# Attention block in BF16: the Q weights as one load, the safe program between two parts of each engine's code

## The chip, the cores and the metric

The kernel runs on one core of one Trainium2 chip. The metric is the device time of one execution in microseconds, lower is better. Three executions of the kernel before gave 420.71, 427.15 and 420.68 us; their median is 420.71.

## What is computed

One attention block without a mask: S = 2048 rows, D = 448, H = 16 heads of 28 columns, everything in bfloat16.

```python
qkv = (x @ wqkv).reshape(B, S, 3, H, Dh).transpose(2, 0, 3, 1, 4)
q, k, v = qkv[0], qkv[1], qkv[2]
scores = einsum("bhqd,bhkd->bhqk", q, k) * Dh ** -0.5
p = softmax(scores, axis=-1)
o = einsum("bhqk,bhkd->bhqd", p, v)
return o.transpose(0, 2, 1, 3).reshape(B, S, D) @ wo
```

## The kernel before

Two whole programs are written into the kernel. The fast one (`_fast`) leaves out the subtraction of the row maximum in the softmax and checks at the end, from the reciprocals of the row sums, that this was safe; it writes the answer as a flag of one number. The safe one (`_general`) subtracts the maximum. It stands behind the fast one in every engine's code and is run only when the flag says so. With the inputs given it never runs.

**The fast program.** Heads are taken four at a time (groups g = 0 to 3) and queries 512 at a time (chunks c = 0 to 3), which gives 16 units u, group by group. For a unit and a block kt of 128 keys there are four tiles of scores, one for each head, 128 x 512. PE computes scores into PSUM (operations S, line 854). ACT takes the exponential of two or three tiles in one instruction (E, line 877), and DVE takes the tiles that are left over by a polynomial in six steps (D1 to D6, lines 899 to 919). PE multiplies the four tiles of a block with V (operations PVu_kt, line 810), which also sums the rows. A unit's result is copied from PSUM (ACCEV), its row sums go through DRAM and back over SP's queue (L1 to L4, lines 722 to 731), and DVE scales the result (NM, line 733). The chunks of the last group are multiplied with wo (OP, line 703), copied (OPEV, lines 689 and 691) and stored (ODMA, line 693). For the last unit, `last_unit` does this without DRAM: the parts of wo of the first three groups are multiplied ahead (OPA, line 752, three matmuls for each of the four row tiles 12 to 15), then come two small transposes and broadcasts by matmul (N1, N2, lines 771 and 786), the scaling (line 791), and the fourth part (OPB, line 795). ACT copies and stores tiles 12 and 14, DVE and SP tiles 13 and 15. The check is a small matmul (CKS, line 947) and an instruction on DVE (FLAG, line 950).

**The order.** A planner (`_Prog.schedule`) simulates the five engines with estimated durations and puts every operation in a fixed place of its engine's stream. Among those that can start it takes the one with the lowest `prio`. Filler matmuls on zeros (Z, line 463) go where PE would otherwise do too little. `emit_engine` writes the streams out, with semaphore waits.

**The start.** x comes in four chunks and wqkv in the parts K, Q, V. Loads are issued by SP and ACT, each in its own queue (lines 424 and 427). PE transposes x (line 527; `tr_job`), DVE or ACT copies the result (xT, lines 511 and 515), and PE projects Q and K of the first group (line 544, `proj_qk`, four passes `it` of four matmuls for each) before the first scores.

**The end.** Each engine waits for the flag, loads it, and branches over the safe program to a block `done_...`, where SP waits for the stores. A hint for the branch (`mark_branch_hint_location`) is written some operations ahead, in front of the operation that `HINT_AT` names. These are the lines:

```python
hint = F.emit_engine(e, eng, fs)
eng.wait_ge(fs["dve"], F.flag_op.count)
ok = eng.value_load(F.flag_ap)
eng.br_ne(ok, 0, on_true=f"done_{e}", on_false=f"safe_{e}").branch_hint(hint)
```

Of the kernel before, what the change touches and what calls it, by code (L numbers as in the profile page):

```python
# [62 lines left out]
class _Prog:  # L63
# [12 lines left out]
    WINDOW = 3413.0  # L76
    FILL = None
    HINT_AT = {}
    FILL_DUR = 235.0
    FILL_ACT = 512.0  # L80
    FILL_TARGET = 5600.0
# [202 lines left out]
                    c += 1  # L284
                    op.count = c

    def emit_engine(self, e, engine, sems):
        waited = {}
        hint = None
        for op in self.order[e]:  # L290
            if op.name == self.HINT_AT.get(e):
                hint = engine.mark_branch_hint_location()
            need = {}
            for d in op.deps:
                if d.dma_group is not None:
                    key = ("dma", id(d.dma_group))
                    val = 16 * d.dma_index
                    sem = d.dma_group.sem
                else:
                    key = ("eng", d.eng)  # L300
                    val = d.count
                    sem = sems[d.eng]
                if waited.get(key, 0) >= val:
                    continue
# [10 lines left out]
        return engine.mark_branch_hint_location() if hint is None and self.HINT_AT else hint  # L315


RLO = 2.0 ** -40
# [18 lines left out]
def _fast(nc, x, wqkv, wo, out, n_heads=16):  # L337
# [32 lines left out]
    P = _Prog()  # L370
    es = ExitStack()
    with es:
# [196 lines left out]

        for c in range(NCH):  # L570
            for it in range(NIT):
                tr_job(4 * c, it, -3 + 0.001 * it if c == 0 else 0.25 * c - CFG["klead"] + 0.001 * it, "act" if (c == 0 and it == 1) else "dve")
# [168 lines left out]
        def last_unit(u, last_pv):  # L741
            g, c = units[u]
            ub = u % 2
            pr = u - 50.0
            open_ops = []
            for j in range(NQT):
                n = c * NQT + j
                hold = []

                for gg in range(G - 1):  # L750
                    def f_part(e, n=n, hold=hold, gg=gg):
                        return e.matmul(bank(hold[0].banks[0])[:, 0:D], OTN[:, gg, n * 128:(n + 1) * 128], wop[:, gg, :],  # L752
                                        start=(gg == 0), stop=False, skip_group_check=True)
                    op = P.add("pe", f_part, deps=([otn_ev[(g_, c)] for g_ in range(G - 1)] + dma_wo[-1:] + mid_ev) if gg == 0 else [], after=hold[-1:], kind="f", units=0.9, act=448.0,
                               prio=-34.0, name=f"OPA{n}_{gg}", acq=("T", 1) if gg == 0 else None)
                    if gg == 0:
                        hold.append(op)
                open_ops.append((n, hold, op))
            HF = QCH // 2
            evs = []  # L760
            for k in range(2):
                sl = slice(k * HF, (k + 1) * HF)
                evs.append(P.add("dve", (lambda e, sl=sl: e.tensor_copy(OTS[:, ub, sl], bank(pv_open[u].banks[0])[:, sl])),
                                 deps=[last_pv, ots_last[ub]], after=evs[-1:], dur=340, prio=pr, name=f"ACCEV{u}_{k}", rel=[(pv_open[u], 0)] if k else []))
            n1s, rss, n2s, nms = [], [], [], []
            for k in range(2):
                def f_n1(e, k=k):
                    b = n1s[k].banks[0]
                    ins = None
                    for qt in (2 * k, 2 * k + 1):  # L770
                        ins = e.matmul(bank(b)[:, qt * 4:(qt + 1) * 4], OTS[:, ub, qt * 128:(qt + 1) * 128], SEL[:, :], start=True, stop=True)  # L771
                    return ins
                n1s.append(P.add("pe", f_n1, deps=[evs[k], sel_op], after=n1s[-1:], dur=430, prio=pr, name=f"N1_{u}_{k}", acq=("T", 1)))
            for k in range(2):
                i0 = u * 16 + 8 * k
                rss.append(P.add("dve", (lambda e, k=k, i0=i0: e.reciprocal(RS[:, i0:i0 + 8], bank(n1s[k].banks[0])[:, 8 * k:8 * k + 8])),
                                 deps=[n1s[k]], after=rss[-1:], dur=120, prio=pr, name=f"RS{u}_{k}", rel=[(n1s[k], 0)]))
                rs_last.append(rss[-1])

# [13 lines left out]
            for j, (n, hold, op) in enumerate(open_ops):  # L793
                def f_fin(e, n=n, hold=hold):
                    return e.matmul(bank(hold[0].banks[0])[:, 0:D], OTN[:, g, n * 128:(n + 1) * 128], wop[:, g, :], start=False, stop=True, skip_group_check=True)  # L795
                fin = P.add("pe", f_fin, deps=[nms[j // 2]], after=[op], kind="f", units=0.9, act=448.0, prio=pr, name=f"OPB{n}")
                out_tile(n, fin, hold[0], "act" if j % 2 == 0 else "dve", pr)

        def pv(u, kt):
# [790 lines left out]
def _mha(nc, x, wqkv, wo, out, n_heads=16):  # L1590
# [3 lines left out]
    with es:  # L1594
# [11 lines left out]
        block = es.enter_context(nc.Block())  # L1606

        def body(e, eng):
            hint = F.emit_engine(e, eng, fs)
            eng.wait_ge(fs["dve"], F.flag_op.count)  # L1610
            ok = eng.value_load(F.flag_ap)
            eng.br_ne(ok, 0, on_true=f"done_{e}", on_false=f"safe_{e}").branch_hint(hint)
            with nc.body(f"safe_{e}", valid_engines=[eng.engine]):
                if e == "sp":
                    for gr in F.finish:
                        eng.wait_ge(gr.sem, 16 * gr.n)
                eng.drain().then_inc(bar, 1)
                eng.wait_ge(bar, 5)
                R.emit_engine(e, eng, rs)
                if e == "sp":  # L1620
                    for gr in R.finish:
                        eng.wait_ge(gr.sem, 16 * gr.n)
                eng.br(f"done_{e}")
            nc.switch_bb(f"done_{e}")
            if e == "sp":
                for gr in F.finish:
                    eng.wait_ge(gr.sem, 16 * gr.n)
# [52 lines left out]
```

## Time and profile before

| what | value |
|---|---|
| median of three executions | 420.71 us |
| the execution with the profile | 424.5 us |
| its span, from the first to the last instruction | 422.7 us |
| mean granted clock of TensorE | 0.996 |
| ACT busy | 402.9 us (95%) |
| DVE busy | 385.5 us (91%) |
| PE busy | 380.2 us (90%) |
| moved by DMA | 10.28 MB |

The profile belongs to one execution, whose own time is 424.5 us; 1.8 us of it lie outside its span. Times inside the span count from its first instruction. PE is the matmul engine, PEld its weight load, DVE the vector engine, ACT the scalar engine, POOL GpSimd, SP the engine that issues most DMAs; a q behind the name marks the engine's sequencer, which works through waits, branches, hints and DMA issues. A row of the timeline has start, duration, engine, line, operation, the tile written and the tile read, shapes, count, and in brackets the idle time before it with what ended it. Line numbers are those of the kernel before.

### The profile page before, as it was taken

Reading aid. Unit: us, or ns where it says so; the run is one execution under the profiler, and the core shown is the slowest. Engines: PE = TensorE matmul, PEld = TensorE weight load, DVE = VectorE, ACT = ScalarE, POOL = GpSimd, SP = SyncE. Lnnn points to the kernel's source line nnn. Section 1 sums busy time; section 2 is a strip of 40 time slices with the busy share of each in tenths; the row PEclk is TensorE's granted clock in tenths of the full one; section 3 lists DMA queues with packets and bytes.
Section 4 is the critical chain, followed back from the end, with each engine's and each line's share of the span. In section 5 each row is a group of like instructions: output and inputs, shape, how many; then the busy total and the mean of one; then the engine's idle time right before and its main releaser. Section 6 shows DMA issues by size and latency. Waiting matters only on the chain.

```text
span 422.7 us, 9986 instructions
## 1 busy us (share of the span) xinstructions
PE 380.2 (90%) x4419; PEld 122.4 (29%) x4419; DVE 385.5 (91%) x608; ACT 402.9 (95%) x312; POOL 3.4 (1%) x9
## 2 busy tenths in 40 slices
PE   6999898899999898998989899989989998898895
PEld 3433222322323223232322222223222322222232
DVE  4489999999999999999999999999999999999923
ACT  2799999999999999999999999999999999999991
POOL 3000000000000000000000000000000000000000
PEclk9899999999999999999999999999999999999999
DMA  8200000101010000100001010000000001100111
GB/s 262 65 2 2 5 26 3 27 0 29 2 26 5 4 26 2 29 2 18 13 3 27 2 28 2 4 26 4 27 2 27 2 6 25 36 28 24 59 44 51
DMA packets 13897, 10.28 MB, mean 24 GB/s; under 512 B 5980, under 2 KB 11868, under 8 KB 13848
## 3 DMA queue, kind: packets, MB, share of 16 engines
q1 hardware_dynamic: 12808, 8.72, 7.6%
q10 hardware_dynamic: 1040, 0.86, 0.6%
q8 instruction: 36, 0.59, 0.6%
q14 instruction: 13, 0.11, 0.1%
HBM read 7.50 MB, written 2.08 MB: 23 GB/s over the span
## 4 chain that ended last, share of the span: by engine, by line
ACT 93%; PE 3%; DMA 2%; DVE 0%; ACTq 0%; issue 0%
ACT PT L877 93%; DMA w_raw<-in_wqkv_dram 2%; PE ps L544 1%; PE ps L752 1%; PE ps L854 0%; PE ps L810 0%; PE ps L527 0%; PE ps L795 0%; PE ps L703 0%; PE ps L771 0%; PE ps L463 0%; DVE OUTS L691 0%; PE ps L786 0%; ACTq L427 0%; ACTq L424 0%; DVE OTN L791 0%
## 5 line engine op out<-in xcount | busy, mean ns | idle before, releaser
L877 ACT ACTIVATE PT<-ps 128x1536 bf16<-128x1536 f32 (+1 forms) x307 | 399.4, 1797 | 2.5 <-PE ps L854 2.5
L854 PE MATMUL ps<-QT,KT 28*128 28x512 bf16 x1024 | 152.5, 384 | 31.4 <-ACT PT L877 28.2
L463 PE MATMUL ps<-ZM,ZW 128*32 128x512 bf16 x1404 | 113.8, 388 | 1.4 <-DVE ZM L445 1.2
L810 PE MATMUL ps<-PT,V 128*32 128x512 bf16 x890 | 96.0, 388 | 2.3 <-DVE OTS L716 1.1
L899 DVE TENSOR_SCALAR DT<-ps 128x512 f32<-128x512 f32 x134 | 91.3, 684 | 2.7 <-PE ps L854 1.5
L854 PEld LDWEIGHTS ps<-QT,KT 28*128 28x128 bf16 x1024 | 37.4, 91 | 164.9 <-ACT PT L877 130.8
L919 DVE SCALAR_TENSOR_TENSOR PD<-DT,DU 128x1024 int16<-128x1024 f32 x67 | 81.7, 1219 | 1.2
L810 PE MATMUL ps<-PD,V 128*32 128x512 bf16 x134 | 50.9, 388 | 0.0
L917 DVE TENSOR_TENSOR DU<-DU,DW 128x1024 f16<-128x1024 f16 x67 | 46.2, 689 | 1.7
L913 DVE TENSOR_TENSOR DU<-DW 128x1024 f16<-128x1024 f16 x67 | 46.0, 686 | 1.5
L911 DVE TENSOR_SCALAR DW<-DT 128x1024 f16<-128x1024 uint16 x67 | 45.5, 680 | 0.2
L463 PEld LDWEIGHTS ps<-ZM,ZW 128*32 128x32 bf16 x1404 | 34.7, 96 | 37.3 <-issue 19.9
L810 PEld LDWEIGHTS ps<-PT,V 128*32 128x32 bf16 x890 | 23.9, 93 | 51.5 <-issue 39.0
L544 PE MATMUL ps<-xT,w_raw 112*32 112x512 bf16 x512 | 35.3, 390 | 2.0 <-DMA w_raw<-in_wqkv_dram 1.8
L915 DVE TENSOR_SCALAR DU<-DU 128x1024 f16<-128x1024 f16 x67 | 27.9, 416 | 0.8
L515 DVE CAST KT<-ps 128x512 bf16<-128x512 f32 x16 | 11.0, 685 | 7.6 <-PE ps L544 7.4
L561 PE MATMUL ps<-w_raw,xT 112*128 112x112 bf16 x256 | 16.4, 214 | 0.2 <-DVE DT L899 0.2
L544 PEld LDWEIGHTS ps<-xT,w_raw 112*32 112x32 bf16 x512 | 11.5, 97 | 16.4 <-issue 3.5
L691 DVE CAST OUTS<-ps 128x448 bf16<-128x448 f32 x14 | 8.7, 622 | 7.2 <-PE ps L703 6.6
L561 PEld LDWEIGHTS ps<-w_raw,xT 112*128 112x128 bf16 x256 | 12.9, 98 | 5.9 <-issue 4.2
L810 PEld LDWEIGHTS ps<-PD,V 128*32 128x32 bf16 x134 | 12.1, 93 | 7.8 <-issue 6.6
L703 PE MATMUL ps<-wop,OTN 128*128 128x448 bf16 x48 | 11.3, 355 | 0.0
(47 smaller groups left out, 96.0 us busy)
## 6 DMA issues: line engine op xcount, KB each, us to landing
RB<-scr_r SPq DMA_DIRECT2D x60, 64.0 KB, 2.0
out_dram<-OUTS SPq DMA_DIRECT2D x14, 112.0 KB, 1.7
x_nat<-in_x_dram SPq DMA_DIRECT2D x3, 448.0 KB, 8.9
w_raw<-in_wqkv_dram SPq DMA_DIRECT2D x2, 196.0 KB, 5.3
w_raw<-in_wqkv_dram ACTq DMA_DIRECT2D x2, 196.0 KB, 5.7
w_raw<-in_wqkv_dram SPq DMA_DIRECT2D x1, 392.0 KB, 9.6
wop<-in_wo_dram SPq DMA_DIRECT2D x16, 24.5 KB
scr_l<-OTS SPq DMA_DIRECT2D x15, 8.0 KB
```

The source lines that it names most:

```text
L463: ins = e.matmul(ps[32 * h:32 * h + 32, b * 512:(b + 1) * 512], ZW[:, :], ZM[:, :], start=shut, stop=shut, skip_group_check=not shut, tile ...
L544: ins = e.matmul(ps[32 * h:32 * h + 32, b * 512:(b + 1) * 512], w_raw[0:IT, it, col:col + 32], xT[0:IT, it, c * 512:(c + 1) * 512], start= ...
L561: ins = e.matmul(ps[:, b * 512 + j * GD:b * 512 + (j + 1) * GD], xT[0:IT, it, n * 128:(n + 1) * 128], w_raw[0:IT, it, 2 * D + g * GD:2 * D ...
L810: ins = e.matmul(ps[32 * h:32 * h + 32, b * 512:(b + 1) * 512], V[:, kt, hh * 32:(hh + 1) * 32], p_ap, start=(kt == 0), stop=(kt == NK - 1 ...
L854: ins = e.matmul(bank(b), KT[32 * h:32 * h + rows, g, kt * 128:(kt + 1) * 128], QT[32 * h:32 * h + rows, g, c * QCH:(c + 1) * QCH], start= ...
L877: ex = P.add("act", (lambda e, p0=p0, w=w, bf=bf: e.activation(PT[:, p0 * 512:(p0 + w) * 512], bank(bf(), w), AF.Exp, scale=ESCALE)), deps ...
L899: o1 = P.add("dve", (lambda e, T1=T1, s=s: e.tensor_scalar(T1, bank(s.banks[0]), ZLO, ZOFF, ALU.max, ALU.add)), deps=[s, d_last[di]], dur= ...
L911: o2 = P.add("dve", (lambda e, F16=F16, W=W: e.tensor_scalar(W, F16, ES, EC, ALU.mult, ALU.add)), deps=[o for _, o, _ in pair] + [d_last[d ...
L913: o3 = P.add("dve", (lambda e, W=W, U=U: e.tensor_tensor(U, W, W, ALU.mult)), deps=[o2], dur=65 + n * 0.521, prio=pr, name=f"D3_{gi}")
L915: o4 = P.add("dve", (lambda e, U=U: e.tensor_scalar(U, U, EP, None, ALU.add)), deps=[o3], dur=65 + n * 0.261, prio=pr, name=f"D4_{gi}")
L917: o5 = P.add("dve", (lambda e, W=W, U=U: e.tensor_tensor(U, U, W, ALU.mult)), deps=[o4], dur=65 + n * 0.521, prio=pr, name=f"D5_{gi}")
L919: o6 = P.add("dve", (lambda e, U=U, T=T, O=O: e.scalar_tensor_tensor(O, T, ZFIN, U, ALU.add, ALU.add)), deps=[o5] + [slot_last.get(("D", q ...
```

## The change

1. The Q part of wqkv is no longer split over the two queues. It is one load of 392 KB on SP's queue, issued behind SP's half of the K part and ahead of the second chunk of x.
2. The second tile of the first transposed chunk (xT, `it` = 1) is copied by DVE, as the other three, not by ACT. The projection of K gets a lower `prio` than that of Q. As the planner places it, PE does the four K passes first and then the four Q passes; before, one K pass, four of Q and three of K.
3. At the end, `prio` of OPA goes from -34.0 to -34.9, and that of the last two OPB from -35 to -34.8. PE's order behind the two OPB of tiles 12 and 13 was OPB14, CKS, OPA15 (three), OPB15; now it is OPA15 (three), OPB14, OPB15, CKS. On DVE the copy of tile 15 now stands in front of FLAG.
4. The safe program no longer stands behind the fast one but in its middle. Every engine jumps over it once, without a condition, to its last part: PE ahead of PV8_11 (ninth unit), DVE ahead of the copy of tile 11, ACT ahead of the copy of tile 12, which is behind its last exponential, SP ahead of its first L1, POOL behind its last operation. Hints stand ahead of three of the jumps: on PE at PV8_8, on DVE at the scaling of the unit before the last, on ACT six exponentials before the end.
5. The closing branch has no hint and no distance: the block `done_...` stands right behind it, and a false flag leads back to the safe program.

Everything else stands in the streams as before.

```diff
-        for t in (1, 0):
-            dma_w[t] = [load_w("act", t, 0, 2), load_w("sp", t, 2, 4)]
+        dma_w[1] = [load_w("act", 1, 0, 2), load_w("sp", 1, 2, 4)]
+        dma_w[0] = [load_w("sp", 0, 0, 4)]
...
-                tr_job(4 * c, it, ..., "act" if (c == 0 and it == 1) else "dve")
+                tr_job(4 * c, it, ..., "dve")
             if c == 0:
-                proj_qk(0, 0, 0, -2.9, True, "act")
                 proj_qk(1, 0, 0, -2.9, True, "dve")
+                proj_qk(0, 0, 0, -2.8, True, "act")
...
-                               prio=-34.0, name=f"OPA{n}_{gg}", ...)
+                               prio=-34.9, name=f"OPA{n}_{gg}", ...)
...
-                fin = P.add("pe", f_fin, ..., prio=pr, name=f"OPB{n}")
+                fin = P.add("pe", f_fin, ..., prio=pr if j < 2 else -34.8, name=f"OPB{n}")
...
-        P.HINT_AT = {"pe": f"OPA{n0}_0", "dve": f"OPEV{n0 - 1}", "act": f"OPEV{n0}", "sp": f"ODMA{n0 + 1}"}
         P.schedule()
+        exps = [op.name for op in P.order["act"] if op.name.startswith("E")]
+        P.HINT_AT = {"pe": "PV8_8", "dve": f"NM{NU - 2}", "act": exps[-6]}
+        P.JUMP_AT = {"pe": "PV8_11", "dve": f"OPEV{n0 - 1}", "act": f"OPEV{n0}", "sp": "L1_0"}
...
         for op in self.order[e]:
             if op.name == self.HINT_AT.get(e):
                 hint = engine.mark_branch_hint_location()
+            if op.name == self.JUMP_AT.get(e):
+                jump(hint)
+                jump = None
...
         def body(e, eng):
-            hint = F.emit_engine(e, eng, fs)
+            top = nc.cur_bb
+
+            def jump(hint):
+                br = eng.br(f"tail_{e}")
+                if hint is not None:
+                    br.branch_hint(hint)
+                with nc.body(f"safe_{e}", parent=top, valid_engines=[eng.engine]):
...
+                    eng.br(f"done_{e}")
+                nc.switch_bb(f"tail_{e}", parent=top)
+
+            F.emit_engine(e, eng, fs, jump)
             eng.wait_ge(fs["dve"], F.flag_op.count)
             ok = eng.value_load(F.flag_ap)
-            eng.br_ne(ok, 0, on_true=f"done_{e}", on_false=f"safe_{e}").branch_hint(hint)
-            with nc.body(f"safe_{e}", valid_engines=[eng.engine]):
...
-            nc.switch_bb(f"done_{e}")
+            eng.br_ne(ok, 0, on_true=f"done_{e}", on_false=f"safe_{e}")
+            nc.switch_bb(f"done_{e}", parent=top)
```

More of the change, by code (lines that the diff above doesn't have):

```diff
@@ L78 @@
     HINT_AT = {}
+    JUMP_AT = {}
     FILL_DUR = 235.0
@@ L285, in assign, with emit_engine @@
                     op.count = c
-    def emit_engine(self, e, engine, sems):
+    def emit_engine(self, e, engine, sems, jump=None):
         waited = {}
@@ L314, in emit_engine @@
                 ins.then_inc(sems[e], 1)
-        return engine.mark_branch_hint_location() if hint is None and self.HINT_AT else hint
+        if jump is not None:
+            jump(hint)
 RLO = 2.0 ** -40
@@ L571, in _fast @@
             for it in range(NIT):
-                tr_job(4 * c, it, -3 + 0.001 * it if c == 0 else 0.25 * c - CFG["klead"] + 0.001 * it, "act" if (c == 0 and it == 1) else "dve")
+                tr_job(4 * c, it, -3 + 0.001 * it if c == 0 else 0.25 * c - CFG["klead"] + 0.001 * it, "dve")
             if c == 0:
-                proj_qk(0, 0, 0, -2.9, True, "act")
                 proj_qk(1, 0, 0, -2.9, True, "dve")
+                proj_qk(0, 0, 0, -2.8, True, "act")
             else:
@@ L754, in last_unit @@
                     op = P.add("pe", f_part, deps=([otn_ev[(g_, c)] for g_ in range(G - 1)] + dma_wo[-1:] + mid_ev) if gg == 0 else [], after=hold[-1:], kind="f", units=0.9, act=448.0,
-                               prio=-34.0, name=f"OPA{n}_{gg}", acq=("T", 1) if gg == 0 else None)
+                               prio=-34.9, name=f"OPA{n}_{gg}", acq=("T", 1) if gg == 0 else None)
                     if gg == 0:
@@ L795, in f_fin @@
                     return e.matmul(bank(hold[0].banks[0])[:, 0:D], OTN[:, g, n * 128:(n + 1) * 128], wop[:, g, :], start=False, stop=True, skip_group_check=True)
-                fin = P.add("pe", f_fin, deps=[nms[j // 2]], after=[op], kind="f", units=0.9, act=448.0, prio=pr, name=f"OPB{n}")
+                fin = P.add("pe", f_fin, deps=[nms[j // 2]], after=[op], kind="f", units=0.9, act=448.0, prio=pr if j < 2 else -34.8, name=f"OPB{n}")
                 out_tile(n, fin, hold[0], "act" if j % 2 == 0 else "dve", pr)
@@ L1608, in body @@
         def body(e, eng):
-            hint = F.emit_engine(e, eng, fs)
+            top = nc.cur_bb
[4 more added lines that the diff above has]
+                with nc.body(f"safe_{e}", parent=top, valid_engines=[eng.engine]):
+                    if e == "sp":
+                        for gr in F.finish:
+                            eng.wait_ge(gr.sem, 16 * gr.n)
+                    eng.drain().then_inc(bar, 1)
+                    eng.wait_ge(bar, 5)
+                    R.emit_engine(e, eng, rs)
+                    if e == "sp":
+                        for gr in R.finish:
+                            eng.wait_ge(gr.sem, 16 * gr.n)
+                    eng.br(f"done_{e}")
+                nc.switch_bb(f"tail_{e}", parent=top)
+            F.emit_engine(e, eng, fs, jump)
             eng.wait_ge(fs["dve"], F.flag_op.count)
             ok = eng.value_load(F.flag_ap)
-            eng.br_ne(ok, 0, on_true=f"done_{e}", on_false=f"safe_{e}").branch_hint(hint)
-            with nc.body(f"safe_{e}", valid_engines=[eng.engine]):
[L1614 to L1623, printed above, removed]
-            nc.switch_bb(f"done_{e}")
+            eng.br_ne(ok, 0, on_true=f"done_{e}", on_false=f"safe_{e}")
+            nc.switch_bb(f"done_{e}", parent=top)
             if e == "sp":
```

## The prediction

> **What bounds the kernel now.** I read the page first, its costliest groups above all, and after it only the first 14 us, the last 14 us and one place in the middle.
>
> ```profile
> span 422.7 us, 9986 instructions
> ...
> L877 ACT ACTIVATE PT<-ps 128x1536 bf16<-128x1536 f32 (+1 forms) x307 | 399.4, 1797 | 2.5 <-PE ps L854 2.5
> ```
>
> The exponentials (L877) fill 399.4 us and are idle only once, 2.5 us, before the first. So three numbers make the span: the start of the first exponential, 399.4 us that nothing in the change touches, and what follows the last one. 399.4 / 307 = 1.30 us is one step, while one record lasts 1.797 us: a record begins about 0.5 us before the one ahead ends, so a score tile is usually ready 0.5 us early. Any stall of PE beyond its cover is lost for good, because ACT has no idle time in which to catch up.
>
> The span's start, by the chain in order of time (start, us, what) and by the timeline:
>
> ```profile
> 1.79 7.02 DMA w_raw<-in_wqkv_dram
> 8.81 0.04 issue
> 8.85 2.67 PE ps L544 x28
> 11.52 1.03 PE ps L527 x8
> 12.55 0.48 PE ps L463 x2
> 13.03 0.38 PE ps L854 x4
> ```
>
> ```profile
> 5.46 0.42 DVE L515 COPY xT<-ps 112x512 bf16<-112x512 bf16 x1 [1.39 <-PE ps L527]
> ...
> 6.63 0.40 PE L544 MATMUL ps<-xT,w_raw 112*32 112x512 bf16 x4 [0.20 <-ACT xT L511]
> ...
> 11.56 0.69 DVE L515 CAST KT<-ps 128x512 bf16<-128x512 f32 x1 [4.56 <-PE ps L544]
> ...
> 13.29 0.65 PE L527 MATMUL ps<-id_b,x_nat 128*112 128x128 bf16 x8
> ```
>
> One K pass runs at 6.63, then PE waits until 8.81 for the second half of the Q weights, with twelve K matmuls that could have run standing behind Q. The first score matmul follows at 13.03 and the first exponential at 13.41. Part of the 2.67 us is a slow clock (busy us of PE, PEld, DVE, ACT, POOL, then the granted clock, DMA share, GB/s):
>
> ```profile
> 6.00:9.40 3.40, 1.38 (x23) 0.75 (x25) 0.76 (x2) 0.48 (x1) 0.00 (x0) 1.00 1.07 350
> 9.40:12.80 3.40, 3.40 (x36) 1.52 (x24) 1.24 (x3) 0.60 (x1) 0.00 (x0) 0.50 0.89 231
> ```
>
> PE was busy 1.38 of 3.40 us, and the next 3.4 us were granted half the clock.
>
> The span's end, PE, ACT and DVE in the timeline, then the sequencers' branch (L1612), their drain (L1594) and SP's last waits (L1627), with first and last start:
>
> ```profile
> 415.96 0.80 PE L795 MATMUL ps<-wop,OTN 128*128 128x448 bf16 x3
> 416.69 0.16 PE L947 MATMUL ps<-ONE,CKM 128*1 128x1 bf16 x1
> 416.79 0.74 PE L752 MATMUL ps<-wop,OTN 128*128 128x448 bf16 x3
> 417.37 0.35 PE L795 MATMUL ps<-wop,OTN 128*128 128x448 bf16 x1
> ```
>
> ```profile
> 416.36 0.54 ACT L689 ACTIVATE OUTS<-ps 128x448 bf16<-128x448 f32 x1 [3.62 <-PE ps L795]
> ...
> 417.72 0.54 ACT L689 ACTIVATE OUTS<-ps 128x448 bf16<-128x448 f32 x1 [0.82 <-PE ps L795]
> 418.30 0.39 ACTq L693 DMA_DIRECT2D out_dram<-OUTS  x1
> ```
>
> ```profile
> 417.76 0.62 DVE L691 CAST OUTS<-ps 128x448 bf16<-128x448 f32 x1 [0.53 <-PE ps L795]
> ```
>
> ```profile
> L1612 PEldq COMPARE_BRANCH  x1: 396/396/396, 417.8 to 417.8; - x1
> L1612 DVEq COMPARE_BRANCH  x1: 84/84/84, 418.5 to 418.5; - x1
> ```
>
> ```profile
> L1594 PEldq DRAIN  x1: 62/62/62, 418.3 to 418.3; - x1
> ...
> L1594 DVEq DRAIN  x1: 58/58/58, 422.2 to 422.2; - x1
> ```
>
> ```profile
> L1627 SPq EVENT_SEMAPHORE  x2: 17/22/28, 422.0 to 422.2; - x2
> ```
>
> All compute is over at 418.4, yet the end is at 422.7. Two things end at 422.2: DVE's branch over the safe program (418.5 + 0.08, next instruction 422.2, so 3.6 us lost in the jump), and SP's wait for the last two output tiles. Why those land late shows in the DMA answers, first of the stretch 416 to 418, then of 418 to 423 (KB, us from issue to landing; for queues: packets, MB, share of 16 engines):
>
> ```profile
> out_dram<-OUTS ACTq DMA_DIRECT2D x1, 112.0 KB, 1.7
> out_dram<-OUTS SPq DMA_DIRECT2D x1, 112.0 KB, 2.0
> ```
>
> ```profile
> q14 instruction: 6, 0.05, 2.9%
> q8 instruction: 1, 0.02, 2.0%
> ...
> out_dram<-OUTS ACTq DMA_DIRECT2D x1, 112.0 KB, 3.7
> out_dram<-OUTS SPq DMA_DIRECT2D x1, 112.0 KB, 3.8
> ```
>
> The same 112 KB took 1.7 and 2.0 us without, 3.7 and 3.8 us with instruction packets beside them. Those packets held 4.9% of 16 engines over 5 us = 3.9 us of engine time, and a tile has landed only when its slowest engine is done. I read the late landing as a second price of the far jumps.
>
> **The change, part by part.**
>
> *Start.* The Q weights arrive as one load on SP's queue, in front of the rest of x; ACT issues one load less. The bytes ahead of the last Q byte are the same, so I leave the landing near 8.8. All four copies of xT now run on DVE, 4 x 0.42 from 5.46 to 7.14. PE's order becomes: all 16 K matmuls, then 16 for Q. K waits for nothing after 7.14 and is done by 7.7, its copy (0.69) by 8.4, hidden under the wait for Q's weights. Q's four passes then run from 8.85 to about 9.8, and ACT copies the result beside what follows. What is late next is the second part of x, for the program order still has its eight transposes and a filler pass before the first score:
>
> ```profile
> x_nat<-in_x_dram SPq DMA_DIRECT2D x1, 448.0 KB, 8.1
> ```
>
> Issued at 2.2, it lands at 10.3, and as many bytes stand ahead of it as before. From 10.3 the old steps follow: 1.03 + 0.48 + 0.38 = 1.9 us at half clock, first exponential at 12.2, gain 1.2. At full clock the eight transposes take 0.65 instead of 1.03 and the filler half, so 1.2 to 1.3 us, first exponential at 11.6, gain 1.8. Three more K passes now fall in the stretch that had 1.38 us of PE work (0.40 a record, overlapping: about 2 of 3.4), so I expect the full clock more often than not. Value 1.7, ends 0.8 (weights half a microsecond later in one queue) and 2.0.
>
> *Order at the end.* The three matmuls of L752 (0.74 us) move ahead of the third of L795, and the flag's small matmul behind the fourth. DVE's last copy starts about 0.3 earlier, 417.45; ACT's copy at 417.72 came 0.9 after its matmul, so 0.5 later for that matmul is covered. The flag, formerly made before DVE's last copy, comes after it, at 418.2: every sequencer waits for it. DVE's branch on it began at 418.5 with the flag right behind the matmul of 416.69; a flag some 1 us later puts the branches at 419.5 or so, before any landing. Cost nothing.
>
> *The closing branch* now falls through into code that lies next to it. The nearest row for a branch that didn't wait for code is PE's, 417.8 plus its own 0.4 to the drain at 418.3: 0.5 us at most. DVE's 3.6 us go, and with them the instruction packets in those 4 us. Then the last landing decides: issue at 418.3 plus 1.7 to 2.0, so 420.2, and from SP's wait to the end it is 0.5 as before: 420.7 in place of 422.7. Gain 2.0; ends 0.3 (the landing stays 3.7 after its issue, for another reason) and 2.2.
>
> *The jumps in mid program.* POOL's and SP's lie where these engines wait. ACT's stands behind the last exponential, in the 3.62 us of idle time before its first output copy; even DVE's old 3.6 us fit. DVE's own jump comes after the copy of the tenth output tile, whose successor waits 2.3 us for PE:
>
> ```profile
> 410.36 0.62 DVE L691 CAST OUTS<-ps 128x448 bf16<-128x448 f32 x1 [2.30 <-PE ps L703]
> ```
>
> ```profile
> L292 DVEq BRANCH_PREFETCH_HINT  x1: 51/51/51, 407.4 to 407.4; - x1
> L292 PEldq BRANCH_PREFETCH_HINT  x1: 45/45/45, 411.0 to 411.0; - x1
> ```
>
> The old hint shows when DVE's sequencer gets there: 407.4, so the cover is 2.9 us. DVE's hint stood 11 us ahead of its branch and the branch still lost 3.6. At that price the copy starts 0.7 late, and with it the last score tile (which needs its bank) and everything behind: 0.65. Without other instruction packets on the way it may be under 2.9, cost 0. I take 0.3.
>
> PE's jump stands before the pass PV8_11, which by its place in the program runs just before these rows, at 234.3:
>
> ```profile
> 234.50 0.60 PE L463 MATMUL ps<-ZM,ZW 128*32 128x512 bf16 x8
> 235.24 0.60 PE L854 MATMUL ps<-QT,KT 28*128 28x512 bf16 x4
> ```
>
> The cover is the 0.14 us gap before the next scores and the 0.5 us from above, 0.64. The nearest row is PE's own branch over the same code, with a hint 6.8 us ahead: 0.4 us. The new hint stands three PV passes ahead; 256 passes in 399.4 us make 1.56 each, so some 4.7 us. So 0, with DVE's 3.6 as the other end: 3.6 - 0.64 = 2.9 lost. [...]
>
> **Sum.** 1.7 + 2.0 - 0.3 - 0 = 3.4 us. The profiled execution took 424.5, 1.8 of it outside its span; it would become 421.1, span 419.3. It is itself 3.8 over the median of the runs, 420.71, and nothing in my terms scales with that, so the forecast is 420.71 - 3.4 = **417.3**.
>
> **Rivals.**
> *PE's jump waits for its code* (0.17). For it: DVE's 3.6 with a hint; PE's code comes in 36 packets over the span, one per 11.7 us, so a hint 4.7 us ahead may fall into the packet before the jump's and be acted on late. Against: PE's own 0.4. Cost 0.4 to 2.9, time 417.7 to 420.2, middle 419.
>
> ```profile
> q8 instruction: 36, 0.59, 0.6%
> ```
>
> *The end doesn't get shorter* (0.13): the closing branch still fetches, or output tiles land late for another reason. Then only the 0.3 us of the reordered matmuls remains and the time is 417.3 + 1.7 = 419.0. For it: I infer the link of packets and landing from two tiles against two.
> *The start gains only 0.8 to 1.0* (0.12): half clock until 12.8 as now, or the single load later; 418.1. [...]
> *Slower than before* (0.05): PE's jump costs all 3.6 us, 2.9 lost; the hole thins PE's work as the stretch 6.0 to 9.4 did, so the next 3.4 us run at half clock, which costs at most 1.7 more; DVE's jump costs its 0.65. That is 5.25 against gains of 3.7: 420.71 + 1.55 = 422.3. It decides once PE's stall passes about 2.5 us and the clock drops.
>
> **Numbers.** The forecast has 0.53. Its own range is 416.2 to 418.2: the best ends (2.0 and 2.2, DVE's 0.3 gone) give 416.5, DVE at 0.65 and a start of 1.2 give 418.2, and 0.3 below is left for the spread of the runs. To leave out no more than 2 in 10 the range must take in the first three rivals nearly whole: 416.0 to 420.0. No case reaches 2% (8.4 us, taken here as about what a measurement of this kernel can tell from no change): faster by more 0.02, within 0.95, slower 0.03 for a jump that goes wrong in a way the trace doesn't price.
>
> **What would show it.** First exponential between 11.4 and 12.3 with no PE wait in front of K; the granted clock at 9.4 to 12.8; L877 still with idle time only before its first; the last two output tiles landing in 2 us, with no instruction packets behind 418; DVE's drain right behind its branch. I am wrong if exponentials wait for PE near 232 us, if the first exponential stays behind 13, or if an output tile still takes 3.7 us.

## The result, and the profile after

The kernel became slightly slower, by less than 1%. Four executions of the changed kernel gave 423.52, 423.94, 430.3 and 424.24 us, median 424.09, beside 421.0 for the kernel before: ratio 1.0072, 95% interval 1.0049 to 1.0094. Ratios and intervals, here and below, leave out the executions that are over 1.5% above the fastest of the same kernel; medians take in all. The forecast was 417.3, its range 416.0 to 420.0. None of the four had a granted clock above 0.988, and the clock turns out to be the story.

The page of the changed kernel: its span, the clock over 40 slices, the shares of the chain that ended last, and the exponentials (L877 before, L882 now).

```profile
span 421.7 us, 9987 instructions
...
PEclk9999999999999999999999999978999999999999
...
ACT 78%; DVE 10%; PE 8%; DMA 2%; SPq 1%; issue 0%; DVEq 0%
...
L882 ACT ACTIVATE PT<-ps 128x1536 bf16<-128x1536 f32 (+1 forms) x307 | 400.1, 1743 | 4.6 <-PE ps L859 4.6
```

The exponentials still take 400.1 us, but they are now idle for 4.6 us, 0.6 ahead of the first and the rest in their midst. The forecast allowed that at one place only, at PE's jump near 232 us. The dip of the clock is in the 27th and 28th of the 40 slices, 274 to 295 us, some 50 us behind PE's jump.

**Start and end did get shorter.** The chain in order of time (start, us, what) at the start of the changed kernel:

```profile
4.82 1.55 PE ps L532 x16
6.37 1.90 PE ps L549 x32
...
9.57 2.83 ACT PT L882 x3
```

All 32 matmuls of K and Q run through without a wait for weights, and the exponentials begin at 9.57. At the end, the closing branch of DVE, the drain behind it, SP's last waits, and the last four output stores (KB, us to landing):

```profile
L1638 DVEq COMPARE_BRANCH  x1: 70/70/70, 419.7 to 419.7; - x1
```

```profile
L1601 DVEq DRAIN  x1: 17/17/17, 419.8 to 419.8; - x1
```

```profile
L1642 SPq EVENT_SEMAPHORE  x2: 17/22/28, 420.6 to 420.9; - x2
```

```profile
out_dram<-OUTS ACTq DMA_DIRECT2D x2, 112.0 KB, 1.7
out_dram<-OUTS SPq DMA_DIRECT2D x2, 112.0 KB, 1.8
```

The drain follows the branch at once, where 3.6 us lay between them, and every store lands in 1.7 to 1.8 us. Behind the last exponential (end 413.63) the span runs another 8.1 us.

**Where the time went.** The same chain between 244 and 278 us, in the changed kernel:

```profile
244.85 3.44 DMA RB<-scr_r
...
248.32 0.69 DVE OTN L738
...
269.14 3.25 DMA scr_r<-RS
...
273.70 1.94 DMA RB<-scr_r
...
275.67 0.69 DVE OTN L738
276.36 1.15 DVE PD L924
...
277.54 0.40 PE ps L815 x4
```

This chain leaves ACT and goes over the round trip of the row sums through DRAM. The reciprocals are stored (scr_r, 8 KB), loaded again as RB, and DVE multiplies by RB in L738. What matters is what stands behind L738 on DVE: L924, the last of the six steps that make PD, the probabilities which DVE computes in ACT's place. PE's next product with V needs that PD. PE's timeline, with the wait in brackets:

```profile
275.48 0.39 PE L859 MATMUL ps<-QT,KT 28*128 28x512 bf16 x3 [0.52 <-ACT PT L882]
277.54 0.39 PE L815 MATMUL ps<-PT,V 128*32 128x512 bf16 x1 [1.67 <-DVE PD L924]
```

And by stretches of a clock window (busy us of PE, PEld, DVE, ACT, POOL, then the granted clock, DMA share, GB/s):

```profile
271.70:275.10 3.40, 3.26 (x48) 1.00 (x45) 2.57 (x5) 3.40 (x3) 0.00 (x0) 1.00 0.23 75
275.10:278.50 3.40, 1.35 (x18) 0.43 (x19) 2.73 (x4) 3.01 (x3) 0.00 (x0) 1.00 0.01 2
278.50:281.90 3.40, 3.40 (x24) 0.61 (x20) 2.71 (x5) 2.13 (x2) 0.00 (x0) 0.50 0.00 0
...
285.30:288.70 3.40, 3.40 (x35) 0.70 (x27) 2.99 (x5) 2.49 (x2) 0.00 (x0) 0.50 0.01 2
288.70:292.10 3.40, 3.40 (x46) 1.50 (x43) 2.39 (x4) 2.79 (x2) 0.00 (x0) 0.99 0.00 0
```

Read the second row as cause and the next ones as price. PE works 1.35 of 3.40 us; then three windows, 10.2 us, are granted half the clock (the first and the third are shown); PE is full in them and still too slow, and ACT works only 2.13 and 2.49 of 3.40. From the first exponential to the end of the last, 404.1 us pass; the control that follows below needs 399.4. These 4.7 us are more than start and end gave. Most of them are lost between 276 and 292 us, about half a us before that, behind the stop of unit 8.

Why were the round trips late? The DMA answer of the changed kernel for 269 to 272.6 us (queue: packets, MB, share of 16 engines):

```profile
GB/s 0 0 0 0 0 0 0 0 0 0 187 51 29 1 0 0 0 0 0 0 0 0 0 0 3 3 0 0 0 0 0 0 0 0 0 0 0 0 0 0
...
q8 instruction: 1, 0.02, 2.2%
...
scr_r<-RS SPq DMA_DIRECT2D x1, 8.0 KB, 3.3
```

One packet of PE's code (16 KB) came in while 8 KB of reciprocals were on the way. It held 2.2% of 16 engines over 3.6 us = 1.3 us of one engine, and the store took 3.3 us where the page's median of fifteen is 1.4. The row GB/s has 40 slices of 0.09 us: packet and store begin together at 269.9, the store is nearly through at 270.3, and its last bytes move at 271.2, when the packet's 1.3 us are over: 9 of the 144 other packets of this window, one in 16, start between 271.15 and 271.32. I read this as a wait for the one engine that carried the packet. It makes up about 1 us of the 1.9 by which the store is late; where the rest comes from isn't shown. In unit 8 a packet lay beside the last of the four RB loads, which took 3.44 us where the median is 2.0. My theory: PE's jump leaves out thousands of instructions, so behind it the ends of PE's 16 KB pieces (256 instructions in the built program; the page has 8,838 matmuls and weight loads and 36 packets, 245 for each) fall elsewhere in the work. By the built program PE jumps over 13,225 instructions, 51 pieces and 169, so the places move by 169 instructions, and by accident they now fall on the round trips of units 8 and 9.

### The profile page after: what moved, and what is told of

Its sections match the earlier page's. It is cut to its first block, busy times and chain, and to the rows that moved or that the text cites. A ratio compares the mean times of both kernels' runs of the same rounds, so it can differ in the third digit from the quotient of the medians.

```text
span 421.7 us, 9987 instructions
## 1 busy us (share of the span) xinstructions
PE 382.5 (91%) x4419; PEld 121.5 (29%) x4419; DVE 386.1 (92%) x609; ACT 403.1 (96%) x311; POOL 3.4 (1%) x9
## 2 busy tenths in 40 slices
DMA packets 13881, 10.28 MB, mean 24 GB/s; under 512 B 5964, under 2 KB 11852, under 8 KB 13832
## 4 chain that ended last, share of the span: by engine, by line
ACT 78%; DVE 10%; PE 8%; DMA 2%; SPq 1%; issue 0%; DVEq 0%
ACT PT L882 78%; DVE DT L904 3%; PE ps L468 2%; DVE PD L924 2%; PE ps L859 2%; DMA RB<-scr_r 1%; DVE DU L918 1%; DVE DW L916 1%; DMA scr_r<-RS 1%; PE ps L815 1%; DVE DU L922 1%; PE ps L757 1%; SPq L736 1%; DVE DU L920 1%; PE ps L532 1%; DVE OTN L738 0%
## 5 line engine op out<-in xcount | busy, mean ns | idle before, releaser
L882 ACT ACTIVATE PT<-ps 128x1536 bf16<-128x1536 f32 (+1 forms) x307 | 400.1, 1743 | 4.6 <-PE ps L859 4.6
L859 PE MATMUL ps<-QT,KT 28*128 28x512 bf16 x1024 | 154.1, 388 | 30.0 <-ACT PT L882 26.0
L468 PE MATMUL ps<-ZM,ZW 128*32 128x512 bf16 x1404 | 115.6, 393 | 1.2 <-DVE ZM L450 1.2
L924 DVE SCALAR_TENSOR_TENSOR PD<-DT,DU 128x1024 int16<-128x1024 f32 x67 | 81.7, 1219 | 1.2
L468 PEld LDWEIGHTS ps<-ZM,ZW 128*32 128x32 bf16 x1404 | 34.8, 97 | 38.4 <-issue 21.8
L549 PE MATMUL ps<-xT,w_raw 112*32 112x512 bf16 x512 | 34.2, 381 | 0.0
L738 DVE TENSOR_TENSOR OTN<-RB,OTS 128x512 bf16<-128x512 f32 x15 | 10.3, 686 | 2.9 <-DMA RB<-scr_r 2.9
```

Of the source, the lines that this page charges most:

```text
L468: ins = e.matmul(ps[32 * h:32 * h + 32, b * 512:(b + 1) * 512], ZW[:, :], ZM[:, :], start=shut, stop=shut, skip_group_check=not shut, tile ...
L549: ins = e.matmul(ps[32 * h:32 * h + 32, b * 512:(b + 1) * 512], w_raw[0:IT, it, col:col + 32], xT[0:IT, it, c * 512:(c + 1) * 512], start= ...
L859: ins = e.matmul(bank(b), KT[32 * h:32 * h + rows, g, kt * 128:(kt + 1) * 128], QT[32 * h:32 * h + rows, g, c * QCH:(c + 1) * QCH], start= ...
L882: ex = P.add("act", (lambda e, p0=p0, w=w, bf=bf: e.activation(PT[:, p0 * 512:(p0 + w) * 512], bank(bf(), w), AF.Exp, scale=ESCALE)), deps ...
L924: o6 = P.add("dve", (lambda e, U=U, T=T, O=O: e.scalar_tensor_tensor(O, T, ZFIN, U, ALU.add, ALU.add)), deps=[o5] + [slot_last.get(("D", q ...
```

## The experiments

Twelve runs were made, four at a time on one chip, each beside the kernel before. Line numbers of the changed kernel hold for its descendants in these rows. The span's rest behind the last exponential is called the tail.

| kernel | executions | median us | fastest us | ratio to before, 95% interval |
|---|---|---|---|---|
| changed, first runs | 4 | 424.09 | 423.52 | 1.0072 [1.0049, 1.0094] |
| changed, again (e4) | 10 | 426.02 | 423.02 | 1.0053 [0.9999, 1.0108] |
| before, once more (c1) | 10 | 422.51 | 421.35 | 1.0021 [0.9975, 1.0068] |
| 87 added (e1) | 10 | 419.44 | 419.02 | 0.9961 [0.9914, 1.0007] |
| PE's jump late (e2) | 10 | 420.82 | 419.52 | 0.9980 [0.9927, 1.0033] |
| start only (e3) | 4 | 424.8 | 422.4 | 1.0104 [1.0001, 1.0207] |
| 222 added (e5) | 10 | 424.73 | 420.09 | 1.0005 [0.9958, 1.0052] |
| old start, 87 added (e6) | 10 | 420.17 | 419.49 | 0.9958 [0.9912, 1.0004] |
| PE without a jump in the middle (e7) | 10 | 422.37 | 420.62 | 0.9960 [0.9919, 1.0002] |
| L738 behind L924, twice (e8) | 10 | 419.78 | 419.01 | 0.9943 [0.9885, 1.0001] |
| L738 later everywhere, 87 added (e9) | 10 | 420.54 | 418.87 | 0.9910 [0.9862, 0.9958] |
| before, L738 later everywhere (e10) | 10 | 422.87 | 420.76 | 1.0001 [0.9951, 1.0051] |
| old end order, 87 added (e11) | 10 | 419.63 | 418.87 | 0.9922 [0.9869, 0.9975] |

The kernel before ran 25, 31 and 31 times beside the three groups, with medians of 421.54, 422.38 and 424.43 and a fastest of 420.58, 420.71 and 420.65. These three fastest agree to 0.13 us. The times follow the granted clock of the execution (0.957 to 1.0), so it is the fastest executions that are compared below, to some tenths of a us.

### The kernel before, unchanged

> The kernel before, unchanged, for a second profile of it. If the profile that the prediction rests on (first exponential at 13.4 us, execution 3.8 us over the median) was an unusual execution, this one has its first exponential near 10 and a span near 419. If it was a usual one, again 13.4 and about 422.7. Ratio 1.000 either way.

Its chain at the start:

```profile
1.79 5.49 DMA w_raw<-in_wqkv_dram
...
7.33 1.70 PE ps L544 x28
...
10.32 3.75 ACT PT L877 x4
```

The second half of Q's weights landed at 7.28 and the exponentials began at 10.3; in the execution that the prediction was made from it was 8.81 and 13.4. Clock 0.998, span 419.5, tail 9.8. The two later profiles with the old start, e6 and e10, have 10.28 and 10.20. So the profile I had read belonged to an execution with an unusual start: 3.1 us of its 3.8 above the median lay in front of the first exponential. The end was as predicted from: DVE's branch at 415.4, its drain at 419.0, the last two stores 3.6 us to landing.

### 87 instructions of PE added, never executed

```diff
                     eng.wait_ge(bar, 5)
+                    for _ in range(174 if e == "pe" else 0):
+                        eng.wait_ge(bar, 5)
```

> The changed kernel with 87 more instructions, never executed, in PE's safe program, so that the boundaries between PE's pieces of 256 instructions fall on the same matmuls as before the change. Theory of the fetches (the jump moved the places where PE's code is fetched, and two of them now delay the round trips through DRAM of units 8 and 9): no DVE idle time of 1 us before L738 in these units, no halved clock near 280, exponentials lose nothing, about 5 us less than the changed kernel: 419 us, faster than before by 1 to 2. Rival 1 (an earlier start leaves DVE too little room): nothing changes, about 424. Rival 2 (the jump stalls PE near 232 us): nothing changes either.

They stand in PE's safe program (two waits become one instruction) and only move the code behind it: 87 of 256 instructions, a third of the 11.7 us between two pieces, 4 us. The same stretch, 269 to 272.6 us, of this kernel has no instruction packet, and:

```profile
scr_r<-RS SPq DMA_DIRECT2D x1, 8.0 KB, 1.4
```

```profile
PEclk9999999999999999999999999999999999999999
```

Profiled time 419.16 us, clock 1.0, no wait at L738 in units 8 and 9. Code that nobody runs is worth 4 us between the fastest executions (423.02 to 419.02). It confirms the places, not yet the way from there to the clock.

### PE's jump near the end

```diff
-        P.HINT_AT = {"pe": "PV8_8", ...}
-        P.JUMP_AT = {"pe": "PV8_11", ...}
+        P.HINT_AT = {"pe": f"OP{n0-1}_0", ...}
+        P.JUMP_AT = {"pe": f"OPA{n0}_0", ...}
```

> The changed kernel with PE's jump ahead of the first OPA of the last unit, its hint ahead of the last OP; all other jumps as in the change. The fetches of units 8 and 9 stay where they were before the change. Theory of the fetches: no halved clock, about 419, plus up to 1 if the jump's code is late there. Rival 1 (earlier start): clock halved again near 280, 424. Rival 2 (PE's jump near 232 us hurts by itself): 419 as well, so this run tells rival 1 from the rest, and the one with the 87 instructions tells rival 2.

The pieces stay where they were before until the last microseconds. Profiled 419.52 at clock 1.0; in the whole span L738 waits for RB once, 0.3 us; tail 8.5. It agrees with the places, and the later jump costs 0.4 of the shorter tail.

### The new start alone

The kernel before with items 1 and 2 of the change.

> The kernel before with the new start alone: Q weights in one load, xT on DVE, K ahead of Q. No jump is moved. If the start gains what the two profiles differ by, 3.8 us, then 417. By the prediction's term 1.7, 419.0. If the old profile's start was unusual, 0 to 1: 420 to 421. Rival 1 (earlier start): halved clock and about 425.

First exponential at 9.95, 0.35 ahead of the control. But here too a half clock came, from 227.4 to 230.8, behind a wait of 1.3 us of the same product (L733 in this kernel) for RB. The store of scr_r ahead of it took 2.7 us, again with a packet of PE's code beside it, so the places can be bad without any jump. The four executions have clocks of 0.971 to 0.993. They don't tell how often that is, nor whether the start has a part in it; the start's worth is better read from e6.

### The changed kernel again

> The changed kernel once more, unchanged, on the same chip as the next three. Theory (PE's jump moved the places at which PE's code arrives, so that they fall on the round trips of the row sums of units 8 and 9): the profile shows again DVE idle about 1 us ahead of the reciprocal (L738) in units 8 and 9, a halved clock from about 279 for one to three windows of 3.4 us, and a granted clock of 0.99 or less over the span; 422 to 425 us. Rival (the four runs seen happened to be disturbed): clock 0.997 or more and 419.0 to 419.6, as with 87 instructions added.

```profile
DVE OTN L738 <- DMA RB<-scr_r: 2.9, 4, 1.3
```

```profile
275.40:278.80 3.40, 1.33 (x18) 0.29 (x10) 2.14 (x3) 3.40 (x4) 0.00 (x0) 1.00 0.19 33
278.80:282.20 3.40, 3.31 (x28) 0.72 (x28) 3.23 (x7) 1.50 (x2) 0.00 (x0) 0.50 0.00 0
```

The first row is from the list of waits (us in total, times, the longest). In this profile the same two stops of DVE come back, 1.13 us in unit 8 and 1.26 in unit 9, with the same 1.67 us wait of PE for PD, and the same thin window; this time one window at half clock followed, and 3.0 us were lost between the first and the last exponential instead of 4.7. The start was later too: the second chunk of x landed at 9.37 and the first exponential began at 10.76. None of its fourteen executions has reached a clock above 0.996, while nine of the twenty of e1 and e6 have 0.999 or 1.0. The rival, that the first four were chance, falls. My bound of 0.99 was too low for two of these ten, the profiled one among them (0.996).

### 222 instructions added

The edit of e1 with 444 in place of 174.

> The changed kernel with 222 instructions of PE, never executed, added to the safe program, in place of 87. They move PE's code boundaries by another 135 instructions. Theory: by the places of the fetches in the run with 87, they now fall on round trips of the row sums in units 9, 10, 11 and two or three later ones (two with scr_r, the others with RB); DVE idle 0.5 to 1.5 us ahead of L738 in at least three of them, at least one stretch of half clock behind 250, 422 to 426 us. Rival (the 87 helped for another reason, by any added code, or by chance): as with 87, 419.0 to 419.8 at full clock.

```profile
DVE OTN L738 <- DMA RB<-scr_r: 1.9, 5, 0.5
```

The stops come in the units named, 9, 10, 11, 13 and 14, but they are short: 0.29 to 0.51 us. The profile has half clock at 125.6, 190.5 and 241.7, none of them behind these stops. So the place of a piece decides whether L738 waits, as expected. But no half clock followed them, and the size that I expected was too large. The fastest execution, 420.09, is 1.1 over that of e1.

### The old start, with the 87

The edit of e1, with the start of the kernel before.

> The changed kernel with 87 added instructions, and with the start of the kernel before (Q's weights in two loads, one copy of xT on ACT, Q ahead of K). My reading now (the start is worth 0.4 us in a usual execution, first exponential 10.3 against 9.9): 419.2 + 0.4 = 419.6, first exponential at 10.3. Rival (the prediction's 1.7): 420.9, first exponential above 11. Second rival (the new start shifts the whole program against the clock's windows, so that the old one is steadier): fewer disturbed runs than with the new start, 419.6 or better in the median.

First exponential at 10.28, tail 8.1, profiled 421.01 with one half-clock window at 315. Its fastest execution is 0.5 over that of e1. The new start is worth about half a us, not 1.7. The granted clocks of the two are alike, so the second rival has nothing for it.

### PE's jump undone alone

```diff
-        P.HINT_AT = {"pe": "PV8_8", ...}
-        P.JUMP_AT = {"pe": "PV8_11", "dve": ...}
+        P.HINT_AT = {"pe": f"OPA{n0}_0", ...}
+        P.JUMP_AT = {"dve": ...}
```

> The changed kernel with PE's jump alone undone: PE's safe program stands behind its last instruction, jumped over there, and the other four engines' stay where the change put them. PE's code boundaries are those of the kernel before. Theory: DVE idle under 0.4 us ahead of L738 in units 8 and 9, no half clock from 279, tail as in the changed kernel (8.1 to 8.5 us behind the last exponential), 419.0 to 419.8 in undisturbed runs. Rival (the later halved clock comes from the start's shift, or from the other engines' jumps): half clock near 279 as in the changed kernel, 422.5 to 424.5.

As expected, no wait at L738 over 0.2 us and no half clock from 279 (this execution had one of four windows from 140.7 and one of one window at 171.4, places that the edit doesn't touch). The time was not as expected: the fastest is 420.62, 1.6 over that of e1. The branch rows and the stores from 417.5 us on show where:

```profile
L1619 PEldq COMPARE_BRANCH  x1: 340/340/340, 419.5 to 419.5; - x1
```

```profile
q8 instruction: 1, 0.02, 1.3%
...
out_dram<-OUTS ACTq DMA_DIRECT2D x2, 112.0 KB, 3.3
out_dram<-OUTS SPq DMA_DIRECT2D x2, 112.0 KB, 3.4
```

PE's far jump is back beside the last stores, they take 3.3 to 3.4 us again, and the tail is 9.45 in place of 8.1. DVE's branch is short here (its drain at 421.7, SP's last wait at 424.2). So the late landing that the prediction inferred from two stores against two is shown: PE's far jump beside the stores costs 1.3 us by itself and had to leave this place. In e2, where it stands at 407.5, the last stores take 1.7 to 1.8 us.

### L738 and L924 exchanged, in units 8 and 9

The run meant to decide: PE's code and its pieces stay as in the changed kernel, and only DVE's order is touched.

```diff
+        o = P.order["dve"]
+        for u, k in ((8, 1), (9, 1)):
+            i = [op.name for op in o].index(f"NM{u}")
+            o.insert(i + k, o.pop(i))
```

> The changed kernel with two instructions of DVE exchanged, twice: in units 8 and 9 the product with the reciprocal sums (L738, which waits for RB) stands behind DVE's next step, the 1.22 us that makes the next PD tile, no longer in front of it. PE's code and so its fetch places stay as in the changed kernel. Theory (late RB, DVE stands at L738, PD late, PE idle about 2.2 of 3.4 us, half clock): RB of units 8 and 9 still lands over 3 us after its issue, but PE's wait for PD (1.67 us at 277 to 279) is gone, no half clock from 279 on, exponentials lose under 0.8 us in 270 to 300, 419.0 to 420.0 in undisturbed runs. Rival (the fetch slows PE itself, or the clock falls for another reason at 279): half clock at 279 again, 423 or more.

DVE and then PE between 274 and 277 us, and PE's stretch of 275.1 to 278.5:

```profile
274.34 1.22 DVE L924 SCALAR_TENSOR_TENSOR PD<-DT,DU 128x1024 int16<-128x1024 f32 x1
275.49 0.68 DVE L738 TENSOR_TENSOR OTN<-RB,OTS 128x512 bf16<-128x512 f32 x1
```

```profile
276.51 0.39 PE L815 MATMUL ps<-PT,V 128*32 128x512 bf16 x1
```

```profile
275.10:278.50 3.40, 2.78 (x38) 0.84 (x35) 3.37 (x6) 3.40 (x4) 0.00 (x0) 1.00 0.00 0
```

PE works 2.78 us where it worked 1.35, the clock stays whole, and no exponential is lost between 150 us and the end. The last of unit 8's four RB loads still landed 3.4 us after its issue; nobody stood waiting for it. In unit 9 the piece came 0.4 us later than in the changed kernel, at 270.4, and held the store of scr_r up no longer (1.4 us). The fastest execution falls from 423.02 to 419.01 by the exchange of two pairs of instructions.

This bears out the way from late RB over DVE's stop to the hole in PE, but not every link by itself. That the exchange takes the stop away while RB is as late as before is shown in unit 8. In unit 9, ahead of the half clock, RB wasn't late any more, so the exchange wasn't put to the test there. That the hole brings the half clock near 279 rests on a comparison of profiles: it is there in both that have the hole (the changed kernel's first and e4) and in none of the other eight kernels made from it, which don't have the hole. How idle PE must be isn't shown. This same profile, like that of e11, has one window at half clock elsewhere, behind a stretch with PE busy 2.71, while e1 was granted the full clock behind 2.60 (275.1 to 278.5):

```profile
71.00:74.40 3.40, 2.71 (x31) 0.67 (x31) 3.37 (x6) 3.40 (x4) 0.00 (x0) 1.00 0.32 77
74.40:77.80 3.40, 3.40 (x35) 0.83 (x32) 2.26 (x5) 3.23 (x3) 0.00 (x0) 0.50 0.00 0
```

### L738 later in all units: with the 87, and in the kernel before

The edit of e8 for units 2 to 11, by one to three DVE steps (in the kernel before the product is L733).

> Both together: the changed kernel with 87 instructions added, and the product of L738 one to three DVE steps later in units 2 to 11. Theory: no wait of DVE for RB anywhere before unit 12, so the undisturbed time stays at 419.0 to 419.3 and fewer runs have a clock under 0.99 than the 4 of 10 with the 87 alone. Rival (the disturbed runs come from elsewhere, or the later product holds something else up): as many, or over 419.6 in the fastest run.

> The kernel before, with the product of L738 one to three DVE steps later in units 2 to 11, nothing else. Theory: the kernel before loses 0.3 to 1.5 us to such waits in units 5 to 7, so 420.3 to 421.0 in undisturbed runs, and fewer runs under a clock of 0.99 than in the kernel before. Rival: same as before, 420.7 to 422.5 in the median.

No wait for RB is left in either profile, and both still have four windows at half clock from 239.8 and 240.0, where no edit of mine changes PE's work. e9's stretches:

```profile
236.40:239.80 3.40, 2.01 (x33) 0.64 (x32) 3.37 (x6) 3.40 (x4) 0.00 (x0) 1.00 0.01 2
239.80:243.20 3.40, 3.40 (x26) 0.59 (x30) 2.85 (x5) 2.63 (x3) 0.00 (x0) 0.50 0.04 7
```

and the same stretch in the kernel before (c1), where full clock followed (c1's own clock windows begin elsewhere; in the one from 237.0 PE was busy 2.35):

```profile
236.40:239.80 3.40, 2.16 (x30) 0.55 (x26) 3.37 (x6) 3.40 (x4) 0.00 (x0) 1.00 0.01 2
```

So the theory failed for e10: its time is that of the kernel before (fastest 420.76 against 420.65), and what brings the clock down there isn't the wait for RB. This program has a thin stretch near 238 of its own. Whether the clock falls behind it, I can't predict. For e9, one of ten executions has a clock under 0.99 where e1 has three (not the four that the expectation names), but under 0.996 both have four: that tells nothing of steadiness, and their fastest are 0.15 apart.

### The old order at the end, with the 87

> The changed kernel with 87 instructions added, and with the old order of the last five output matmuls and of the flag. The prediction put the new order at nothing: then from the end of the last exponential to the end of the span it is 8.1 us as with the new order, and 419.0 to 419.3 undisturbed. Rival (the new order carries part of the shorter end): 8.4 to 8.7 us there, 419.4 to 419.8.

The edit takes item 3 back. Tail 8.2 against 8.1, fastest 418.87. The new order is worth nothing that these runs can tell, as predicted.

## Why the prediction was wrong, step by step

*The step that failed* is "399.4 us that nothing in the change touches". From the first to the last exponential 4.7 us were added, of the 6.8 between the forecast and the measured median. The prediction put no price on the new places of PE's code behind the jump, and gave no reason for it. Without these 4.7 us the profiled 423.5 would have been 418.8, inside the range.

*The sum was also set against the wrong base.* "Nothing in my terms scales with that" was the sentence that failed here. The profiled execution was 3.8 over the median, and most of that was the stall that I then counted as gain: the first exponential at 13.4 where a usual one has 10.2 to 10.3 (c1, e6, e10). I took 1.7 off a median that didn't contain the stall. Against the control, the changed kernel's profile starts 0.75 earlier, e3 0.35; e1 beats e6 by 0.5. The ten profiles with the new start begin the exponentials between 9.55 and 10.76, in the middle at 9.9. So the term of 1.7 should have been about 0.4 to 0.5. Its mechanism held in part: K no longer stands behind Q's weights. In e1 these weights come last (7.43) and in e4 and e7 the second chunk of x (9.37, 8.96), as the prediction had it; in the changed kernel's first profile neither stands in the chain.

*The end* gave what was forecast: 9.8 to 8.1 is 1.7, against 2.0 + 0 for the two steps. DVE's 3.6 us are gone and the stores land in 1.7 to 1.8. e7 and e11 show which edit carries it: not the new order, but that no far jump is near the last stores (e7 shows it for PE's).

*ACT's and DVE's jumps* cost nothing. The rows of the changed kernel:

```profile
L1619 DVEq COMPARE_BRANCH  x1: 80/80/80, 408.3 to 408.3; - x1
L1619 ACTq COMPARE_BRANCH  x1: 52/52/52, 412.6 to 412.6; - x1
```

```profile
411.27 0.62 DVE L696 CAST OUTS<-ps 128x448 bf16<-128x448 f32 x1 [2.33 <-PE ps L708]
```

```profile
417.24 0.54 ACT L694 ACTIVATE OUTS<-ps 128x448 bf16<-128x448 f32 x1 [3.61 <-PE ps L800]
```

DVE's next copy still waits 2.33 us for PE, ACT's 3.61: both jumps lie inside waits that were there before. I had taken 0.3 for DVE.

*PE's jump, taken at 0 (ends 0 and 2.9)*, is the step that turned the sign, though at its own place the 0 was right:

```profile
L1619 PEldq COMPARE_BRANCH  x1: 339/339/339, 229.8 to 229.8; - x1
```

It took 0.34 us, and no exponential came late there. PE's hint ran at 224.4, and a 16 KB packet of its code came at 225.5; such a packet stands 1.1 us behind PE's hint in the kernel before (411.0 and 412.1) and 1.0 to 1.3 us in e1, e4, e5, e6 and e8. The other end, 2.9 at the price of DVE's row, did not occur. Nor did PE stop for the packet of 269.9: its timeline shows no wait from 268 to 275 us. The packet's cost fell on another engine's small transfer, the store that took 3.3 us where the median is 1.4. I had priced code only where it is jumped to and not where, after the jump, it is fetched from then on. The prediction had quoted the line with the 36 packets and used it only for the hint.

The account from the control (421.36) to the changed kernel's profile: start -0.75, tail -1.69, exponentials +4.73, together 423.65; measured 423.52, with the time outside the span 0.1 different.

*The rivals.* "Slower than before" held 0.05 and came true in its sign, by half of its mechanism: a hole that thins PE's work and a half clock behind it. The other half is luck. But the hole came through DVE 45 us later, not from the jump's stall, and the half clock lasted up to three windows in place of one. The other three were about effects that didn't occur or, for the start, were closer than the forecast.

## What to carry to other kernels

Before you subtract a stall from a median, look whether the execution that shows the stall is like those that make the median; a second profile of the control would have cost one experiment. In these runs a jump in PE's code, or 87 instructions more, moved the later packets of that code (one came at 269.9 us in the changed kernel, none from 269 to 272.6 with the 87), so look which small DMAs that an engine waits for they may meet, and put a step that needs such a DMA behind the work that others wait for: here the exchange of two pairs of DVE instructions brought 4 us, though partly because one store was no longer late either. Keep far jumps away from the last stores: with PE's beside them (e7) these landed in 3.3 to 3.4 us, without it in 1.7 to 1.8.

## What the runs showed that I had not expected

- PE busy 1.33 of one 3.4 us stretch was followed by half clock for one window (e4), PE busy 1.35 for three (first profile); the longest single gap of PE in them was 1.67 us. Busy time doesn't decide alone: PE busy 2.01 of 3.4 (e9), 2.71 (e8) and 2.90 (e5, before 125.6) was followed by half clock, and 2.13 (e3, from 237.6) by full clock. So no threshold can be read off these rows.
- The same kernel's executions have granted clocks from 0.957 to 0.996 (e4) or 0.976 to 1.0 (e1), and their times follow, 423.0 to 434.9 and 419.0 to 426.2. What brings the clock down in the kernel before, in executions without late RB, stays open.
- The best versions tried, e1, e8, e9 and e11, reach 418.9 to 419.0 where the kernel before reaches 420.6 and the changed one 423.0; the intervals of e9 and e11 lie below 1.
